# Opening of a state-space and MLP kernel: zero products first, first products split by tokens, one gate pass, and two tiles of B rows transposed by DMA

## Chip, cores and metric

One core of one Trainium2 chip. The metric is the device time of one execution in microseconds, lower is better. The time before is the median of five runs.

## The reference

For each of 2048 tokens `x` (width 1024) two branches are computed and mixed by a gate that is one number per token.

```python
g = _sigmoid((x * gate_w).sum(-1, keepdims=True))

# branch a: a diagonal complex state-space layer
Lam_bar = jnp.exp(dt * Lam)
B_bar = ((Lam_bar - 1.0) / Lam)[:, None] * Bmat
Bu = jnp.einsum("bld,pd->blp", x + 0j, B_bar)
for t in range(L):
    h = Lam_bar[None, :] * h + Bu[:, t, :]
y = 2.0 * jnp.einsum("blp,dp->bld", hseq, Cmat).real + x * Dskip

# branch b: layer norm and an MLP of width 3584
h = _gelu(jnp.einsum("bsd,df->bsf", _layernorm(x), w1) + b1)
b = jnp.einsum("bsf,fd->bsd", h, w2) + b2

out = g * a + (1 - g) * b
```

All inputs and the output are bf16.

## The kernel before

The program is a graph of tasks. Each task belongs to one engine (`pe`, `act`, `dve`, `pool`, or `sp` for DMA issue), has an estimated duration, a priority tuple and the buffers that it reads and writes. A list scheduler in `Graph` plays the graph through with those estimates and so fixes one order of instructions for each engine; on the chip every engine works through its order and waits on semaphores where a task needs another engine's or a DMA's result. Smaller priority tuples go first. A changed estimate (`DMAT_BW` is the assumed rate of transposing DMAs, `slack` an assumed delay of one task's input) changes the orders and nothing else.

The stages, in the order of the priorities:

1. **The opening.** `x` (tiles of 128 tokens) and `B_re`, `B_im` (tiles of 128 state channels, "p tiles") are needed with the width on the partitions. Tokens 0 to 511 are loaded as they are (`load_x`), transposed on TensorE (`t_x`, line 646) and copied out of PSUM by VectorE (line 650). The natural B rows of p tiles 0 to 3 are loaded to the region `RX` (`load_b0`, `load_b`), transposed on TensorE (`t_b`, line 662) and copied out by ScalarE (line 666). The other tokens come by DMA transposes of 512 tokens, 1 MB each (`xT_dma`, line 990), the B rows of p tiles 4 to 7 by DMA transposes of 256 KB (`bT_dma`, line 1079). The buffers of transposed B rows form a ring of five, `BQ`; the last two of them lie over `RX`.
2. **Constants.** Small vectors are loaded to `stg` (line 575), transposed in one TensorE instruction (line 693) and turned into the decay, its powers and tables by a long chain of small VectorE instructions with a few ScalarE functions (lines 696 to 814).
3. **Input products.** `bu_plain` computes the products of p tiles 0 and 1 with 512 tokens directly: eight matmuls of 512 columns for each part (real, imaginary), accumulated in one of six PSUM banks, which ScalarE empties (line 925). All later groups (`bu_group`) use a scheme with seven products of half-size blocks in place of eight (class `SG`, steps `p1` to `p7`): VectorE first forms sums of blocks (`b_sums` for B, `x_sums` for x with `ut1` to `ut4`; line 895), ScalarE copies or seeds partial results (lines 850 and 867). `ut4` and `bs4` are written over a block that the plain products read. The order of groups (p tile, token half) is (2,0), (3,0), (0,1), (1,1), ...
4. **Gate rows.** `z_gate` multiplies the columns `gate_w` and ones with x; the results of four token chunks lie in four strips of partitions of PSUM bank 7. It is done once for each token half (line 1046), ScalarE copies the rows out (line 1053), `z_move` sends them through DRAM to get one number per token on the partitions (lines 1062 and 1067). The ones give the sums for the layer norm. Later ScalarE applies tanh (line 1122) and VectorE makes `G` and `GM1`.
5. **Layer norm** (`ln_stats`; squares on ScalarE, line 1001; the norm on VectorE, line 1021), stored and read back by transposing DMAs.
6. **MLP**: blocks `m` (first product, gelu at lines 1295 and 1301) and `b` (second product, scaled by `GM1` at lines 1378 and 1381), accumulated in DRAM.
7. **The state recurrence** `ssm` (lines 1162 to 1189): filler work for VectorE with low priority between all these, 16 units of multiply, scan, multiply.
8. **The last stage** `y`: eight groups of the product with C, combined with the gate, the skip term and the MLP result (lines 1458 to 1480), and stored.

TensorE's instructions of the opening are chained one after the other in program order:

```python
t_x(0, (-0.8, 0), 7, [])
t_x(1, (-0.8, 1), 3, last_pe())
t_b(0, (-0.8, 2), (0,), (1, 2), last_pe())
t_x(2, (-0.8, 3), 0, last_pe())
t_x(3, (-0.8, 4), 7, last_pe())
t_b(0, (-0.79, 0), (1,), (1, 2), last_pe())
```

SyncE issues, in this order: x tiles 0 and 1, B re of p tile 0, x tiles 2 and 3, B im of p tile 0, the natural rows of p tiles 1 to 3, three DMA transposes of x, then x tiles 4 to 15 (for the layer norm) with the transposes of p tile 4 among them.

Of the kernel before, what the change touches and what calls it, by code (L numbers as in the profile page):

```python
# [7 lines left out]
F32 = mybir.dt.float32  # L8
# [14 lines left out]
DMAT_BW = 150e3  # L23
# [396 lines left out]
def build(nc, A_x, A_Lambda_re, A_Lambda_im, A_B_re, A_B_im, A_C_re, A_C_im, A_log_dt, A_Dskip,  # L420
# [25 lines left out]
    with es:  # L446
# [110 lines left out]
        for nm in ("SUM", "SSQ", "MEAN", "EX2", "MSQ", "VAR", "RSTD", "NMR", "Z", "TZ", "G", "GM1"):  # L557
            alloc_cols(nm, NTT)
# [20 lines left out]
        g.dma(P0, emit_cst_loads, NROW * 256, sem("d_cst"), writes=[b_stg], name="cst_loads", ndma=len(vecs), q="act")  # L579
# [73 lines left out]
        def t_b(pt, prio, ris=(0, 1), bks=None, ex=()):  # L653
            s = pt % 4
            for ri in ris:
# [8 lines left out]
                g.add("pe", 0.06 * DT, prio, em, reads=[AR.v(RX + s * 4096 + ri * 2048, [(1, D)]), b_ident], writes=[b_ps[bk]], name="bT%d.%d" % (pt, ri), extra=ex)  # L664
                o = AR.v(bqo(pt, 2 * ri), [(1, D)])
                first_a.append(g.add("act", c_act(D), prio, lambda e, o=o, bk=bk: e.activation(o.ap, V(PS16[bk], 0, [(1, D)]), AF.Copy),
                                     reads=[b_ps[bk]], writes=[o, b_ps[bk]], name="bTe%d.%d" % (pt, ri)))

        def load_b0(ri, ap):
            v = AR.v(RX + ri * 2048, [(1, D)])  # L670
            g.dma((-0.9, 1.5 + 2 * ri), lambda e: e.dma_start(out=v.ap, in_=ap[0:128, :]), 128 * D * 2,
                  sem("d_b0%d" % ri), writes=[v], name="bnat0.%d" % ri)

        load_b0(0, A_B_re)
        load_b0(1, A_B_im)
        BN[0] = AR.v(RX, [(1, 2 * D)])
        for k in range(4):
            load_x(k, (-0.9, k))
        for pt in range(1, 4):
            load_b(pt, (-0.85, pt))  # L680
# [4 lines left out]
        t_x(0, (-0.8, 0), 7, [])  # L685
        t_x(1, (-0.8, 1), 3, last_pe())
        t_b(0, (-0.8, 2), (0,), (1, 2), last_pe())
        t_x(2, (-0.8, 3), 0, last_pe())
        t_x(3, (-0.8, 4), 7, last_pe())
        t_b(0, (-0.79, 0), (1,), (1, 2), last_pe())  # L690
# [33 lines left out]
        dv("cos", lambda e: e.activation(C("C1", 0, n8), C("T3", 0, n8), AF.Sin, scale=TWO_PI), ["T3"], ["C1"], dur=0.3, eng="act", prio=P0)  # L724
        dv("ur0", lambda e: e.tensor_tensor(C("UR", 0, n8), C("R", 0, n8), C("C1", 0, n8), ALU.mult), ["R", "C1"], ["UR"])
# [189 lines left out]
        def bu_plain(pt, c):  # L915
# [4 lines left out]
            for ri in range(2):  # L920
                bk = (4, 5, 6, 0, 1, 2)[nxt("cbank", 6)]
                ws = [AR.v(bqo(pt, 2 * ri) + dt * 256, [(1, 128)]) for dt in range(DT)]
                q = mm("bu%d.%d.%d" % (pt, c, ri), bk, ws, [xt(dt, c) for dt in range(DT)], True)
# [6 lines left out]
        def b_sums(pt, q):  # L930
            def bv(i, dt=FP16):
                return AR.v(bqo(pt, i), [(1, 512)], dt)
            dve_tt("bs1_%d" % pt, q, bv(4), bv(2, BF16), bv(3, BF16), ALU.add, 512)
            dve_tt("bs2_%d" % pt, q, bv(5), bv(4), bv(0, BF16), ALU.subtract, 512)
            dve_tt("bs3_%d" % pt, q, bv(6), bv(0, BF16), bv(2, BF16), ALU.subtract, 512)
            dve_tt("bs4_%d" % pt, q, bv(2), bv(1, BF16), bv(5), ALU.subtract, 512)

        def x_sums(pr, q):
            def xv_(i, dt=FP16):
                return AR.v(xqo(pr, i), [(1, 2048)], dt)  # L940
            dve_tt("ut1_%d" % pr, q, xv_(4), xv_(2, BF16), xv_(0, BF16), ALU.subtract, 2048)
            dve_tt("ut2_%d" % pr, q, xv_(5), xv_(3, BF16), xv_(4), ALU.subtract, 2048)
            dve_tt("ut3_%d" % pr, q, xv_(6), xv_(3, BF16), xv_(2, BF16), ALU.subtract, 2048)
            dve_tt("ut4_%d" % pr, q, xv_(2), xv_(1, BF16), xv_(5), ALU.subtract, 2048)
# [52 lines left out]
        def ln_stats(c, prio):  # L997
            for i in range(TT):
# [3 lines left out]
                      reads=[xv], writes=[v_j, bc("SSQ%d" % k)], name="ln_sq%d" % k, extra=[first_a[3]])  # L1002
# [34 lines left out]
        def z_gate(pr):  # L1037

            cs = (2 * pr, 2 * pr + 1)
            xs = [[xt(dt, c) for c in cs] for dt in range(DT)]  # L1040

            def em(e):
                ins = None
                for dt in range(DT):
                    for i, c in enumerate(cs):
                        ins = e.matmul(bass.AP(PS[7], 32 * c * 512, [[512, 2], [1, CH]]), V(GWC, 2 * dt, [(1, 2)]), xs[dt][i].ap, start=(dt == 0), stop=(dt == DT - 1))
                return ins
            seq[0] += 1
            t = g.add("pe", 1.0, (1.0, seq[0]), em, reads=xs + [b_gwc], writes=[b_ps[7]], name="z%d" % pr, extra=pe_last)
            pe_last[:] = [t]  # L1050
            for c in cs:
                o = bass.AP(AR.h[F32], 32 * c * zrow + ZR // 4, [[zrow, 2], [1, CH]])
                g.add("act", c_act(CH), (1.0, seq[0]), lambda e, c=c, o=o: e.activation(o, bass.AP(PS[7], 32 * c * 512, [[512, 2], [1, CH]]), AF.Copy),
                      reads=[b_ps[7]], writes=[zr, b_ps[7]], name="ze%d" % c)

        def z_move(pr):

            prio = (1.0, seq[0])
            n = NTT // 2

            def em_st(e):
                return [e.dma_start(out=ZS[r, pr * 1024:(pr + 1) * 1024].rearrange("(c t) -> c t", c=2),
                                    in_=bass.AP(AR.h[F32], (64 * pr + r) * zrow + ZR // 4, [[32 * zrow, 2], [1, CH]])) for r in range(2)]
            g.dma(prio, em_st, L * 4, sem("d_zst%d" % pr, True), reads=[zr], writes=[b_zs[pr]], name="zst%d" % pr, ndma=2, q="pool").slack = 0.5
# [610 lines left out]
```

## Time and profile before

| | |
|---|---|
| median of 5 runs | 566.86 us (563.22 to 576.39) |
| the profiled execution's own time | 565.94 us |
| its span, first to last instruction | 564.2 us |
| TensorE busy in the span | 545.5 us |
| VectorE busy in the span | 519.9 us |
| ScalarE busy | 288.1 us |
| POOL busy | 94.6 us |
| first TensorE instruction | 3.32 us |
| HBM read, written | 60.98 MB, 48.38 MB |

Lines of the timeline read: start, length, engine, line of the kernel, operation, tiles written and read, shapes, count; in brackets the idle time of the engine before it and what ended it. Neighbouring instructions of one line are merged into one row. PE is TensorE's matmul, PEld its weight load, DVE VectorE, ACT ScalarE, SPq SyncE's DMA issue. A busy TensorE is not one at its best pace: the duration of like instructions has to be compared too.

### The profile page before, as it was taken

The page shows a single profiled execution, that of the slowest core. Times are in us where ns is not written, and L with a number is a line of the kernel's source. Part 1 is how long each engine was busy: PE and PEld are TensorE (multiplying, and loading weights), DVE is VectorE, ACT ScalarE, POOL GpSimd, SP SyncE. Part 2 cuts the span into 40 slices and gives each one's busy share as a digit, 9 for nine tenths or more (in the row PEclk, how much of TensorE's full clock was granted, in tenths as well). Part 3 has the DMA queues.
Part 4 walks back from the last instruction along what each step waited for, and adds up shares of the span by engine and source line. Part 5 has one row for each costly group of instructions (what it writes and reads, how often), then busy time and mean ns, then how long its engine had stood idle before and what let it go on. Part 6 is the DMA issues. An engine that isn't in the chain of part 4 may idle for free. (4 is left out here: it accounts for less than half of the span.)

```text
span 564.2 us, 7415 instructions
## 1 busy us (share of the span) xinstructions
PE 545.5 (97%) x2553; PEld 249.8 (44%) x2601; DVE 519.9 (92%) x894; ACT 288.1 (51%) x481; POOL 94.6 (17%) x153
## 2 busy tenths in 40 slices
PE   6999999989999999999999999999999999999995
PEld 5544444434444444444444444444444444444442
DVE  4899989999999999999999999999999788999952
ACT  3969989667774247774347663347663331111110
POOL 0225736530001110001110001120001110010100
PEclk9999999999999999999999999999999999999998
DMA  8995999767882564303998997997699799788421
GB/s 268 241 313 123 259 266 275 263 216 217 268 186 94 212 218 147 114 0 128 341 379 275 354 256 177 242 196 243 195 236 173 160 295 361 261 323 313 151 108 56
DMA packets 122287, 125.58 MB, mean 223 GB/s; under 512 B 70530, under 2 KB 99970, under 8 KB 121226
## 3 DMA queue, kind: packets, MB, share of 16 engines
q1 hardware_dynamic: 109136, 77.23, 48.9%
q0 software_dynamic: 13008, 47.87, 27.6%
q8 instruction: 20, 0.33, 0.2%
q14 instruction: 17, 0.14, 0.1%
q10 hardware_dynamic: 106, 0.02, 0.0%
HBM read 60.98 MB, written 48.38 MB: 194 GB/s over the span
## 5 line engine op out<-in xcount | busy, mean ns | idle before, releaser
L833 PE MATMUL ps<-ar 128*128 128x512 f16 (+1 forms) x1792 | 412.1, 379 | 6.1 <-ACT ar L850 1.6
L833 PEld LDWEIGHTS ps<-ar 128*128 128x128 f16 (+1 forms) x1832 | 178.5, 98 | 222.2 <-ACT ar L850 3.2
L831 PE MATMUL ps<-ar 128*128 128x512 bf16 (+1 forms) x632 | 156.2, 380 | 1.6 <-DVE ar L895 1.0
L895 DVE TENSOR_TENSOR ar<-ar 128x512 f16<-128x512 bf16 (+7 forms) x244 | 150.5, 652 | 7.4 <-DMA ar<-in_A_B_im_dram 2.4
L831 PEld LDWEIGHTS ps<-ar 128*128 128x128 bf16 (+1 forms) x640 | 62.2, 98 | 76.9 <-DVE ar L895 2.4
L1176 DVE TENSOR_TENSOR_SCAN ar<-cst,init,ar 128x256 bf16<-128x256 f32 x128 | 88.7, 734 | 0.4
L850 ACT ACTIVATE ar<-ps 128x512 f32<-128x512 f32 x100 | 58.8, 594 | 50.2 <-PE ps L831 37.7
L1162 DVE TENSOR_TENSOR ar<-ar 128x2048 bf16<-128x2048 bf16 x64 | 77.0, 1216 | 0.1
L867 ACT ACTIVATE ps<-ps 128x512 f32<-128x512 f32 x66 | 38.5, 583 | 68.2 <-PE ps L831 50.1
L1295 ACT ACTIVATE ar<-ps,cst 128x512 bf16<-128x512 f32 x56 | 38.4, 686 | 22.1 <-PE ps L833 21.4
L851 ACT ACTIVATE ar<-ps,cst 128x512 f32<-128x512 f32 x32 | 22.0, 687 | 45.5 <-PE ps L833 23.4
L1301 ACT ACTIVATE ar<-ar,cst 128x512 bf16<-128x512 f32 x56 | 40.0, 715 | 7.7 <-DVE ar L1299 7.7
L1378 ACT ACTIVATE ar<-ps,cst 128x512 f32<-128x512 f32 x32 | 22.0, 687 | 40.8 <-PE ps L833 40.8
L1165 DVE TENSOR_TENSOR ar<-ar 128x1024 bf16<-128x1024 bf16 x64 | 42.3, 684 | 0.3
L1299 DVE TENSOR_TENSOR ar<-ps,ar 128x512 f32<-128x512 f32 x56 | 38.2, 683 | 3.5 <-PE ps L833 3.1
L910 POOL DMA_DIRECT2D scr_u<-ar x32 | 24.9, 780 | 40.7 <-DVE ar L976 17.5
L1480 DVE SCALAR_TENSOR_TENSOR ar<-ps,cst,ar 128x512 bf16<-128x512 f32 x32 | 23.8, 745 | 7.4 <-PE ps L833 7.4
L1390 POOL DMA_DIRECT2D scr_ac<-ar x16 | 13.7, 859 | 88.4 <-DVE ar L1381 54.1
L1381 DVE SCALAR_TENSOR_TENSOR ar<-ps,cst,ar 128x512 f32<-128x512 f32 x32 | 23.7, 740 | 3.8 <-PE ps L833 3.7
L1388 POOL DMA_DIRECT2D scr_ac<-ar x16 | 8.5, 532 | 100.4 <-DVE ar L895 89.2
L1194 POOL DMA_DIRECT2D scr_h<-ar x16 | 9.3, 584 | 86.6 <-DVE ar L1165 86.5
L1487 POOL DMA_DIRECT2D out_dram<-ar x14 | 7.6, 544 | 84.3 <-DVE ar L1480 84.3
(104 smaller groups left out, 260.0 us busy)
## 6 DMA issues: line engine op xcount, KB each, us to landing
scr_ac<-ar POOLq DMA_DIRECT2D x32, 512.0 KB, 6.3
ar<-in_B_w_dram SPq DMA_DIRECT2D x21, 512.0 KB, 5.5
ar<-in_A_x_dram SPq DMA_DIRECT2D x32, 256.0 KB, 6.5
scr_u<-ar POOLq DMA_DIRECT2D x32, 256.0 KB, 4.9
ar<-scr_u SPq DMA_DIRECT2D x16, 512.0 KB, 5.0
scr_h<-ar POOLq DMA_DIRECT2D x16, 512.0 KB, 5.4
ar<-scr_h SPq DMA_DIRECT2D x8, 1024.0 KB, 7.2
ar<-scr_ac SPq DMA_DIRECT2D x16, 512.0 KB, 7.7
```

The costliest lines, as they stand in the source:

```text
L831: ins = e.matmul(V(PS[bk], 0, [(1, n)]), st[i].ap, mv[i].ap, start=(i == 0), stop=(i == K - 1))
L833: ins = e.matmul(V(PS[bk], 0, [(1, n)]), st[i].ap, mv[i].ap, start=False, stop=(i == K - 1), skip_group_check=True)
L850: return e.activation(o.ap, V(PS[bk], 0, [(1, 512)]), AF.Copy)
L867: g.add("act", c_act(512), (pb[0], q - 2), lambda e: e.activation(V(PS[b], 0, [(1, 512)]), V(PS[a], 0, [(1, 512)]), AF.Copy), reads=[b_ps[ ...
L895: g.add("dve", c_tt16(n), (pb[0], q), lambda e: e.tensor_tensor(o.ap, a.ap, b.ap, op), reads=[a, b], writes=[o], name=nm, extra=ex).slack ...
L910: g.dma((1.0, q), lambda e: e.dma_start(out=US[pt // 4, :, 4 * pr:4 * pr + 4, r0:r0 + T], in_=evv.ap), 2 * 128 * CH * 2, ssem("us", 2 * ks ...
L1162: g.add("dve", c_tt16(UE), pri(i), lambda e: e.tensor_tensor(o.ap, a.ap, tbl.ap, ALU.mult), reads=[a, tbl], writes=[o], name=nm + tag)
L1165: g.add("dve", c_tt16(UE // 2), pri(i), lambda e: e.tensor_tensor(o.ap, a.ap, b.ap, op), reads=[a, b], writes=[o], name=nm + tag)
L1176: lambda e, pt=pt, ri=ri, vin=vin, go=go: e.tensor_tensor_scan(go.ap, Cb("R", pt, T), vin.ap, V(INIT, pt * 2 + ri, [(1, 1)]), ALU.mult, AL ...
L1295: g.add("act", c_act(512, ap_operands=1), (10.0, q + 1), lambda e: e.activation(o.ap, V(PS[bk], 0, [(1, 512)]), AF.Gelu_apprx_tanh, bias=C ...
L1299: g.add("dve", c_dve(512), (10.0, q - 2), lambda e: e.tensor_tensor(sv.ap, V(PS[bk], 0, [(1, 512)]), sv.ap, ALU.add), reads=[b_ps[bk], sv] ...
L1301: g.add("act", c_act(512, psum=False, ap_operands=1), (10.0, q + 3), lambda e: e.activation(o.ap, sv.ap, AF.Gelu_apprx_tanh, bias=C("B1", ...
```

## The change

- Loads: B re of p tile 0 is issued first, then x tiles 0 and 1, B im, x tiles 2 and 3, and the natural rows of p tile 1. Those of p tiles 2 and 3 are no longer loaded; their transposed rows come by `bT_dma`, between the DMA transposes of x. The constants' loads go from ScalarE's queue to POOL's.
- TensorE's opening begins with six products of zeros; the direct products of p tile 0 with the first 512 tokens are done in halves of 256 tokens between the transposes (`part`). The PSUM copies of p tile 0's rows are shared by VectorE and ScalarE.
- The gate rows of all four token chunks are made in one pass within group (3,0), `ut4` of the first token half after it.
- The gate's tanh is replaced by a power of e on POOL and a reciprocal on VectorE; a small gelu instruction stands early in ScalarE's order.
- The scheduler's numbers: a higher rate for transposing DMAs, and 5 us of slack for two of the four B sums of p tiles above 4.

```diff
-DMAT_BW = 150e3
+DMAT_BW = 200e3
...
-        g.dma(P0, emit_cst_loads, NROW * 256, sem("d_cst"), writes=[b_stg], name="cst_loads", ndma=len(vecs), q="act")
+        g.dma((-0.5, 0), emit_cst_loads, NROW * 256, sem("d_cst"), writes=[b_stg], name="cst_loads", ndma=len(vecs), q="pool")
...
+                w = D // 2 if halves else D
+                if halves:
+                    o = AR.v(bqo(pt, 2 * ri) + D, [(1, w)])
+                    g.add("dve", 0.36, prio, lambda e, o=o, bk=bk: e.tensor_copy(o.ap, V(PS16[bk], w, [(1, w)])),
+                          reads=[b_ps[bk]], writes=[o, b_ps[bk]], name="bTd%d.%d" % (pt, ri))
+                o = AR.v(bqo(pt, 2 * ri), [(1, w)])
...
-        load_b0(0, A_B_re)
-        load_b0(1, A_B_im)
+        for k, ri in ((None, 0), (0, None), (1, None), (None, 1), (2, None), (3, None)):
+            if ri is None:
+                load_x(k, (-0.9, k + 1 if k < 2 else k + 2))
+            else:
+                load_b0(ri, (A_B_re, A_B_im)[ri])
         BN[0] = AR.v(RX, [(1, 2 * D)])
-        for k in range(4):
-            load_x(k, (-0.9, k))
-        for pt in range(1, 4):
-            load_b(pt, (-0.85, pt))
+        load_b(1, (-0.85, 0))
...
+        v_zero = AR.v(B2B, [(1, CH)])
+        g.add("dve", 0.1, (-2.0, 0), lambda e: e.memset(v_zero.ap, 0.0), writes=[v_zero], name="zero")
+
+        def warm(n, bk, w):
+            def em(e):
+                ins = None
+                for i in range(n):
+                    ins = e.matmul(V(PS[bk], 0, [(1, w)]), AR.v(B2B, [(1, 128)]).ap, AR.v(B2B, [(1, w)]).ap, start=True, stop=True)
+                return ins
+            g.add("pe", n * w * 0.00084, (-0.8, -1), em, reads=[v_zero], writes=[b_ps[bk]], name="warm", extra=last_pe())
+
+        def part(t0, n, ri):
+            if True:
+                ws = [AR.v(bqo(0, 2 * ri) + dt * 256, [(1, 128)]) for dt in range(DT)]
+                xs = [AR.v(xqo(0, 0) + dt * 1024 + 2 * t0, [(1, n)]) for dt in range(DT)]
+                bk = 4 + ri
...
+                        ins = e.matmul(V(PS[bk], t0, [(1, n)]), ws[dt].ap, xs[dt].ap, start=(dt == 0), stop=(dt == DT - 1))
...
-        t_x(0, (-0.8, 0), 7, [])
+        warm(6, 6, CH)
+        t_b(0, (-0.8, 2), (0,), (1, 2), last_pe(), True)
+        t_x(0, (-0.8, 0), 7, last_pe())
         t_x(1, (-0.8, 1), 3, last_pe())
-        t_b(0, (-0.8, 2), (0,), (1, 2), last_pe())
+        t_b(0, (-0.8, 2), (1,), (1, 2), last_pe(), True)
+        part(0, 256, 0)
         t_x(2, (-0.8, 3), 0, last_pe())
         t_x(3, (-0.8, 4), 7, last_pe())
-        t_b(0, (-0.79, 0), (1,), (1, 2), last_pe())
+        part(0, 256, 1)
+        part(256, 256, 0)
+        t_b(1, (-0.8, 5), (0,), (1, 2), last_pe())
+        part(256, 256, 1)
+        t_b(1, (-0.8, 5), (1,), (1, 2), last_pe())
...
+        g.add("act", 0.3, (3.0, 0), lambda e: e.activation(C("KF2", 0, 1), C("MHALF", 0, 1), AF.Gelu_apprx_tanh), ... name="gelu_tab")
...
+            sl = 5.0 if pt > 4 else 0.0
+            dve_tt("bs1_%d" % pt, q, bv(4), bv(2, BF16), bv(3, BF16), ALU.add, 512, sl)
...
+            dve_tt("bs3_%d" % pt, q, bv(6), bv(0, BF16), bv(2, BF16), ALU.subtract, 512, sl)
...
-        def z_gate(pr):
+        def z_gate():
...
-                    for i, c in enumerate(cs):
-                        ins = e.matmul(bass.AP(PS[7], 32 * c * 512, [[512, 2], [1, CH]]), V(GWC, 2 * dt, [(1, 2)]), xs[dt][i].ap, start=(dt == 0), stop=(dt == DT - 1))
+                    for c in range(NCH):
+                        ins = e.matmul(bass.AP(PS[7], 32 * c * 512, [[512, 2], [1, CH]]), V(GWC, 2 * dt, [(1, 2)]), xs[dt][c].ap, start=(dt == 0), stop=(dt == DT - 1))
...
-        for pt in range(1, 4):
-            t_b(pt, (0.9, pt))
-        for c in range(1, NCH):
-            xT_dma(c, (-0.6 + 0.1 * c, 0))
...
+        xT_dma(1, (-0.84, 0))
...
+        bT_dma(2, (-0.83, 0))
+        bT_dma(3, (-0.35, 0))
+        xT_dma(2, (-0.4, 0))
+        xT_dma(3, (-0.3, 0))
...
-            if c == 1:
-                z_gate(0)
-                z_move(0)
             for pt in range(2):
                 bu_plain(pt, c)
-        x_sums(0, seq[0])
+        x_sums(0, seq[0], (0,))
...
             if (pt, pr) == (0, 1):
-                z_gate(1)
-                z_move(1)
                 x_sums(1, seq[0])
...
             cur.p6()
+            if n == 1:
+                z_gate()
+                z_move()
+                x_sums(0, seq[0], (1,))
             cur.p2()
...
-        g.add("act", 0.3, (5.0, 0), lambda e: e.activation(C("TZ", 0, NTT), C("Z", 0, NTT), AF.Tanh, scale=0.5), ...
+        g.add("pool", 0.5, P0, lambda e: e.memset(C("EULER", 0, NTT), 2.718281828459045), writes=[bc("EULER")], name="euler")
...
+        gp("nz", lambda e: e.tensor_scalar(C("TZ", 0, NTT), C("Z", 0, NTT), -1.0, 0.0, ALU.mult, ALU.add), zb, "TZ")
+        gp("ez", lambda e: e.tensor_tensor(C("EZ", 0, NTT), C("EULER", 0, NTT), C("TZ", 0, NTT), ALU.pow), [bc("TZ"), bc("EULER")], "EZ")
+        gp("e1", lambda e: e.tensor_scalar(C("TZ", 0, NTT), C("EZ", 0, NTT), 1.0, 0.0, ALU.add, ALU.add), [bc("EZ"), bc("TZ")], "TZ")
+        g.add("dve", 0.1, (5.0, 0), lambda e: e.reciprocal(C("G", 0, NTT), C("TZ", 0, NTT)), reads=[bc("TZ")], writes=[bc("G")], name="G")
```

## The prediction

> **What bounds the kernel now.** I read the page first, then the table of windows, the timeline of the opening, the waits, and the chain that ended last.
>
> ```profile
> PE 545.5 (97%) x2553; PEld 249.8 (44%) x2601; DVE 519.9 (92%) x894; ACT 288.1 (51%) x481; POOL 94.6 (17%) x153
> ...
> DVE  4899989999999999999999999999999788999952
> ```
>
> TensorE is busy 545.5 of 564.2 us, so 18.7 us is all its idle time: 3.3 before the first transpose, some 6.8 after the last product, and the rest in a few gaps. Nothing outside TensorE's own work can give much. VectorE is the second bound: nine tenths or more in nearly every slice, with little room when TensorE gets quicker.
>
> ```profile
> 3.32 1.03 PE L646 MATMUL ps<-ident,ar 128*128 128x128 bf16 x8 [3.32 <-DMA ar<-in_A_x_dram]
> ...
> 7.12 1.91 PE L646 MATMUL ps<-ident,ar 128*128 128x128 bf16 x16
> ...
> 12.34 1.06 PE L662 MATMUL ps<-ident,ar 128*128 128x128 bf16 x16
> 13.23 1.89 PE L831 MATMUL ps<-ar 128*128 128x512 bf16 x8
> 14.96 0.61 PE L662 MATMUL ps<-ident,ar 128*128 128x128 bf16 x8
> ...
> 20.45 1.89 PE L1046 MATMUL ps<-ar,gwc 128*2 128x512 bf16 x16
> 22.27 8.81 PE L831 MATMUL ps<-ar 128*128 128x512 bf16 x39
> 30.98 2.75 PE L833 MATMUL ps<-ar 128*128 128x512 f16 x12
> ```
>
> This is TensorE's opening. Before 10 us sixteen transposes take 1.70 us start to start (7.12 to 8.82); at 12.34 sixteen take 0.89 (12.34 to 13.23). The pace doubles between 10.4 and 12.3 us, after work without a gap since 6.29 (the wait for the first B rows ends there). The stretch at 22.27 holds the last 32 plain products and the first 8 of group (2,0): that group begins at 30.98 - 8 x 0.216 = 29.2 us (0.216: the eight products at 13.23 are followed at 14.96, 1.73 us later).
>
> ```profile
> 100.16 1.28 ACT L1122 ACT_TABLE_LOAD   x1
> ...
> 102.21 1.90 PE L833 MATMUL ps<-ar 128*128 128x512 bf16 x8 [0.90 <-ACT ar L850]
> ...
> 126.28 3.63 PE L833 MATMUL ps<-ar 128*128 128x512 f16 x16 [1.45 <-ACT ps L867]
> ```
>
> ScalarE loads a table for tanh, and TensorE waits 0.90 us behind it. The 1.45 us gap comes some 5 us after the like load for the first gelu (at 120.30).
>
> ```profile
> 430.00:470.00 40.00, 39.79 (x183) 18.09 (x185) 32.67 (x41) 11.35 (x18) 6.53 (x8) 1.00 0.87 218
> 470.00:537.00 67.00, 65.73 (x301) 29.79 (x306) 66.55 (x90) 10.31 (x18) 6.52 (x12) 1.00 0.78 278
> ```
>
> Columns: stretch, length, busy time of PE, PEld, DVE, ACT and POOL, then clock and DMA. From 470 to 537 VectorE has 0.45 us idle; at 521 TensorE waits for it:
>
> ```profile
> 519.15 1.19 DVE ar L1459
> 520.34 0.61 DVE ar L895
> 520.95 0.05 issue
> 521.00 1.90 PE ps L831 x8
> ```
>
> These are pieces of the chain that ended last: it leaves TensorE for VectorE between 510 and 521 us.
>
> **The opening, part by part.** Each load takes SyncE about 0.45 us to issue. The first six land at 3.3, 4.6, 6.25, 7.0, 7.9 and 8.6 us (issue plus time to landing), the next two at 8.95 and 9.9. I keep these times and put the new order on them: B re, x0, x1, B im, x2, x3, B1 re, B1 im.
> Zero products: six of 512 columns at the slow pace (0.106 per 128 columns, so 0.427 each) are 2.6 us, from about 1.0 (first VectorE memset at 0.87) to 3.6. They lie in the 3.3 us wait for the first load and cost 0.3 at most, which the wait for x0 at 4.6 swallows. What they may bring is the early pace. No row shows it, so two ends:
> Slow until 11.3 as now: B re 3.6-4.5, x0 4.6-5.5, x1 6.3-7.15, B im 7.15-8.0, first half product (8 x 0.213) 8.1-9.8, x2 and x3 9.8-11.5, then fast: three half products of 0.88, two transposes of B1 at 0.45, constants 0.15, to 15.2. The 48 plain products left, at 0.216, are 10.4: group (2,0) at 25.6.
> Fast from 4.6: the same list waits for landings and for x1's eviction (0.69 at line 650) until 7.75, ends at 13.3, and group (2,0) begins at 23.7.
> Before, without the first gate pass (1.8), it is 29.2 - 1.8 = 27.4. The gain is 1.8 to 3.7; I take 2.8, the middle. It contains the four transposes of p tiles 2 and 3 that leave (4 x 0.45 to 0.6).
> [...]
>
> Gate rows: 20.45 to 22.27 and 39.70 to 41.53 are 3.65 us for two passes of 16. In one pass two strips already run at the price of one (16 of them in 1.89). Four at once would be 1.8; if the weight loads (16 in 1.38 us, line 1046) bind, 32 take 2.75; with no more overlap than now 3.65. I take 2.2: gain 1.45, ends 0 and 1.85.
> The pass now lies in group (3,0), and ut4 of the first x half, in place over what the pass reads, must follow it. Behind ut4 waits p4 of group (2,0). Cover: p2 and p3, 8 x 0.216 = 1.7 us. ut4 takes 0.96 to 1.22 (line 895, 2048 wide) after at most one such instruction ahead of it: 0 to +1.2, I take +0.2. The pass also waits for all x by DMA: SyncE issues the three 1 MB transposes in 4.8 us each (the first 7.4, behind loads), with two pairs of B rows (1.24 + 1.40 each) between. Two fewer pairs of loads are ahead, so it starts at 4.6, not 6.75: first issue done near 11.9, B2 14.6, second x 19.4, B3 22.0, third x 26.8, landing 2 to 3.5 us later. Wanted: second x chunk at 17 to 19 (lands near 15), B2 at 24, third x at 32 to 33: all covered.
> x4 to x15 and p tile 4's transposes come behind this: x4 is issued near 29.4 instead of 23.8. Cover: the norm that reads them starts at 59.1 and its first product past 114; price if the cover is gone, the 5.6 us.
>
> Moved off queues: five constant loads go from ACT to POOL. POOL takes 0.55 to 0.8 each (lines 1062, 910), so about 1.4 to 5.5, landing by 8.5; the constants' transpose comes at 15. ACT sheds four evictions of 1.03, half of two, three gate evictions of 0.59 and tanh; idle time of ACT, no gain. One cost sits here: the constant chain on VectorE starts at 15.2 instead of 10.1.
>
> **Later parts.** Without tanh, and with gelu's table loaded in the opening (1.28 us, between evictions of 0.6 that come every 1.7 us; without that cover 1.3): the 0.90 gap goes. The 1.45 gap hangs also on VectorE's add ahead of a gelu, so little of it. I take -1.2, ends 0 and -2.35. The planner's 5 us for B sums of p tiles over 4: VectorE waited 2.39 us for a B row at 73.81, TensorE 0.73 after it: -0.3, ends 0 and -0.73. The gate on POOL (three small operations, up to 1.4 each as at line 1015) is due at 166.9, line 1378: nothing.
>
> **VectorE's share.** TensorE would come 5.5 us earlier (2.8 + 1.45 + 1.2), VectorE's chain 5.1 later, and two half copies add 0.7 (half of line 650 each): 11.3 us less room. Idle that lateness fills by itself: its waits for TensorE, 4.9 in 430:470 and about 3.0 between 183 and 424, and the 2.4 of the B row: 10.3. So at least 1.0 returns as TensorE stalls in the 470 to 537 stretch. If VectorE's fixed order regains little of it (about half, 5.4), 5.9 returns. I take +1.6, ends 0 and +5.9.
>
> Sum: -2.8 - 1.45 + 0.2 - 1.2 - 0.3 + 1.6 = -3.95, and +0.3 for p tile 3's B rows, whose margin is thin (below): -3.65. The profiled execution took 565.94 us (span 564.2, 1.7 around it): **562.3 us**, 0.64% less. The median of the runs shown is 566.86, 0.2% above that execution, and the runs reach from 563.22 to 576.39; I don't correct for it. About 1%, 5.7 us, is what a measurement here tells from no change.
>
> **Rivals.** All of it arrives and VectorE keeps up: -3.7 - 1.85 - 2.35 - 0.73 = -8.6, 557.3 us. For it: VectorE idles 7.3 us in 430:470. Against: 0.45 in the stretch after.
> VectorE takes the bound over: -2.8 - 1.45 - 1.2 - 0.3 + 0.5 + 5.9 = +0.65, 566.6 us. For it: the chain through VectorE at 510 to 521. Against: its waits for TensorE go by themselves when it is late.
> Slower: B rows of p tile 3 land late. Their region is that of the natural B rows, so they wait for B1's transposes, and may be issued behind the third x chunk: imaginary row issued near 25.5. Group (3,0) wants its sum at 30.3. At 3.5 us to landing all is well; the longest such landing in the trace is 12.3 (line 1079): 37.8, a stall of 7.5, +3.9 in all, 569.8 us. It decides from a landing after 34.0. For it: the median for imaginary rows is 10.1. Against: those were queued behind ten x loads.
> The zero products may also do nothing to the pace: 563.3, inside the forecast.
>
> **How the numbers follow.** Forecast 0.53, all arrives 0.27, VectorE takes over 0.11, late B rows 0.09. Faster by over 1% (under 560.3): 0.27 and 0.06 of the forecast, 0.33. Slower by over 1%: 0.09, nearly all of the last. Within: 0.58. The range goes from the first rival, 557, to 568, part of the way to the last; the forecast's own is 559.5 to 565.5.
>
> **What would show it.** Right: TensorE's first matmuls near 1 us, transposes at 0.61 per eight before 8 us or at the latest by 11.3, group (2,0) at 23.7 to 25.6, one gate pass of 1.8 to 2.75, no table load after 40 us, 2 to 3 us more TensorE idle in the last 100 us. Wrong: group (2,0) after 27, a gap at group (3,0), a gate pass of 3.6, or VectorE's idle in 430:470 unchanged.

## Result and profile after

The change makes the kernel slower by 0.8%: 572.32 us median (565.02 to 584.24, 44 runs) against 566.25 us (561.02 to 576.39, 79 runs of the kernel before on the same chips). The ratio is 1.008 with a 95% interval of 1.0057 to 1.0104; it leaves out executions that lie far above the fastest of their kernel, which is why it is below that of the medians. The prediction was 562.3 us and at most 568.

The profiled execution took 581.03 us (span 579.3), so it is one of the long ones; a second trace of the same kernel (run e9 below) took 576.37 us (span 574.6) and loses its time in the same places. Lines of the kernel have moved: 646 and 662 (transposes) are the same, 831 and 833 (products) are 872 and 874, 850 and 867 are 891 and 908, 895 is 936, 1046 is 1095, 1219 (the transposing loads of the normed x, called xn here) is 1273, 1480 is 1534. The zero products are line 700, the half products line 714.

Of the page, the sums by engine, VectorE's slices and the granted clock:

```profile
PE 550.4 (95%) x2544; PEld 250.1 (43%) x2591; DVE 522.4 (90%) x897; ACT 280.7 (48%) x473; POOL 99.4 (17%) x160
...
DVE  4899797799999999999988999999999979999853
...
PEclk9999799799999999999999999999999999997998
```

TensorE is now idle 28.9 us (579.3 - 550.4; it was 18.7). The clock row has three dips, at the slices near 65, 110 and 530 us; before, it had none until 560.83 us. VectorE has holes at the same early slices.

The timeline of TensorE's opening:

```profile
1.24 2.74 PE L700 MATMUL ps<-ar 128*128 128x512 bf16 x6 [1.24 <-DVE ar L818]
...
4.63 1.44 PE L646 MATMUL ps<-ident,ar 128*128 128x128 bf16 x16
6.08 0.62 PE L662 MATMUL ps<-ident,ar 128*128 128x128 bf16 x8
...
12.84 12.03 PE L872 MATMUL ps<-ar 128*128 128x512 bf16 x54 [0.16 <-ACT ar L971]
25.70 2.75 PE L874 MATMUL ps<-ar 128*128 128x512 f16 x12 [0.82 <-DVE cst L786]
...
32.87 1.90 PE L1095 MATMUL ps<-ar,gwc 128*2 128x512 bf16 x32 [0.97 <-DMA ar<-in_A_x_dram]
```

The row that stood at 30.98 stands at 25.70, and the 32 gate products take 1.90 us: in this trace the opening did what was forecast. The rival of late B rows didn't occur: the imaginary row of p tile 3 is issued at 20.45, ahead of the third x chunk, and lands at 25.04. TensorE's waits from 60 to 540 us, the three longest:

```profile
PE ps L874 <- ACT ar L891: 6.1, 1, 6.1
PE ps L874 <- DVE ar L1534: 3.8, 1, 3.8
PE ps L874 <- ACT ar L1029: 3.3, 1, 3.3
```

Before, the longest wait in this stretch was 1.45 us. The timeline around the longest, all engines:

```profile
94.61 9.98 SPq L1273 DMA_TRANSPOSE ar<-scr_xn  x2
...
97.48 0.17 DVE L1239 TENSOR_TENSOR fxt<-ar,cst 128x8 f32<-128x8 bf16 x1
...
104.87 1.23 DVE L936 TENSOR_TENSOR ar<-ar 128x2048 f16<-128x2048 bf16 x1 [7.22 <-DMA ar<-scr_xn]
...
107.41 0.60 ACT L1029 ACTIVATE ar<-ps 128x512 f32<-128x512 f32 x1 [6.87 <-DVE ar L1031]
107.90 1.08 ACT L891 ACTIVATE ar<-ps 128x512 f32<-128x512 f32 x2
...
108.55 3.60 PE L874 MATMUL ps<-ar 128*128 128x512 bf16 x8 [6.05 <-ACT ar L891]
```

VectorE comes in its fixed order to the first sum of normed x at 97.65 and waits 7.22 us for the transposing loads. Behind the sum stand the copies that ScalarE and then TensorE wait for. The last row holds a second price: eight products in 3.60 us, 0.43 each where 0.22 is usual. The table of windows shows it:

```profile
103.92:107.34 3.42, 0.00 (x0) 0.00 (x0) 2.47 (x4) 0.00 (x0) 0.35 (x1) 1.00 1.04 208
107.34:110.75 3.41, 2.20 (x6) 0.83 (x7) 3.41 (x6) 2.06 (x4) 2.80 (x5) 0.50 1.14 303
110.75:114.16 3.41, 3.41 (x10) 1.20 (x9) 3.38 (x8) 0.81 (x2) 1.40 (x3) 0.50 0.86 333
```

After the five busy times and their counts comes the granted clock: half for 6.83 us after the gap. TensorE works for 2.20 + 3.41 = 5.61 us of it, so the wait of 6.05 us costs up to half of that, 2.8 us, more (an estimate from the two paces, 0.43 and 0.22).

The table of windows for the two stretches that the prediction watched:

```profile
430.00:470.00 40.00, 39.79 (x183) 18.14 (x186) 39.00 (x54) 12.06 (x18) 6.63 (x8) 1.00 0.86 198
470.00:537.00 67.00, 62.33 (x273) 27.41 (x276) 61.45 (x83) 9.57 (x16) 6.28 (x11) 0.95 0.86 296
```

VectorE's idle time in the first fell from 7.3 to 1.0 us, as lateness would have it; in the second TensorE now idles 4.7 us, where it was 1.3.

By stretches, TensorE's idle time in the first trace before and in e9: 60 to 95 us 0.9 and 2.5, 95 to 110 us 0.95 and 8.9, 470 to 540 us 1.3 and 3.95. That is 12.2 us more. In e9's two half-clock stretches (6.83 and 3.41 us; the granted clock is 0.86 from 95 to 110 us, 0.93 from 110 to 130 and 0.98 from 470 to 540) TensorE is busy for 7.3 us, half of which, 3.6, is lost; together 15.8. The span is only 10.4 longer, so some 5.4 us were gained elsewhere. Against the second trace of the kernel before (e10 below: span 560.0, idle 0.2, 0.2 and 1.5 us in the same stretches) the same sum is 13.5 + 3.6 - 14.6: some 2.5 us gained.

### The profile page after: what moved, and what is told of

Read it like the earlier page. It is cut to its first block, busy times and chain, and to the rows that moved or that the text cites. A ratio compares the mean times of both kernels' runs of the same rounds, so it can differ in the third digit from the quotient of the medians.

```text
span 579.3 us, 7382 instructions
## 1 busy us (share of the span) xinstructions
PE 550.4 (95%) x2544; PEld 250.1 (43%) x2591; DVE 522.4 (90%) x897; ACT 280.7 (48%) x473; POOL 99.4 (17%) x160
## 3 DMA queue, kind: packets, MB, share of 16 engines
q0 software_dynamic: 13104, 47.88, 27.3%
## 4 chain that ended last, share of the span: by engine, by line
PE 69%; DVE 12%; DMA 7%; SPq 5%; POOL 2%; issue 2%; ACT 1%; DVEq 0%; ACTq 0%; POOLq 0%
PE ps L874 54%; PE ps L872 15%; DMA ar<-in_A_x_dram 4%; DMA ar<-in_B_w_dram 2%; DVE ar L936 2%; SPq L1040 2%; DVE ar L1513 2%; DVE ar L1534 2%; SPq L1273 1%; SPq L1123 1%; DVE ar L1532 1%; DMA ar<-scr_xn 1%; DVE ar L1512 1%; DVE ar L1230 1%; DVE ar L1216 1%
## 5 line engine op out<-in xcount | busy, mean ns | idle before, releaser
L874 PE MATMUL ps<-ar 128*128 128x512 f16 (+1 forms) x1799 | 417.7, 383 | 18.4 <-ACT ar L891 6.1
L936 DVE TENSOR_TENSOR ar<-ar 128x512 f16<-128x512 bf16 (+6 forms) x244 | 150.1, 653 | 13.4 <-DMA ar<-scr_xn 7.2
L872 PE MATMUL ps<-ar 128*128 128x512 bf16 (+1 forms) x610 | 153.5, 385 | 1.4 <-DMA ar<-scr_h 0.4
```

The costliest lines, as they stand in the source:

```text
L872: ins = e.matmul(V(PS[bk], 0, [(1, n)]), st[i].ap, mv[i].ap, start=(i == 0), stop=(i == K - 1))
L874: ins = e.matmul(V(PS[bk], 0, [(1, n)]), st[i].ap, mv[i].ap, start=False, stop=(i == K - 1), skip_group_check=True)
L936: g.add("dve", c_tt16(n), (pb[0], q), lambda e: e.tensor_tensor(o.ap, a.ap, b.ap, op), reads=[a, b], writes=[o], name=nm, extra=ex).slack ...
```

## Experiments

All kernels whose part of the change is undone are planned anew by the scheduler, so every engine's order moves with them. Those marked "orders kept" change what an instruction does, or the place of a named few, and nothing else in any engine's order.

**One part undone (e1 to e4).** The planner's rate back, two gate passes, B rows by TensorE, tanh on ScalarE.

```diff
-DMAT_BW = 200e3
+DMAT_BW = 150e3
```

> The changed kernel with one number undone: the planner's rate for transposing DMAs is 150e3 again (it changes engine orders only). Theory R (rate): the higher rate makes the planner place VectorE's sums of the normed x before the transposes that feed them have landed, and VectorE's 7.2 us wait at 105 us and TensorE's 6.05 us gap behind it come from that: without it that gap is under 1.5 us, and the time falls 5 to 9 us below the changed kernel's, to 0.992 to 1.000 of the kernel before. Theory G (one gate pass), theory B (B rows by DMA) and theory P (gate's power on POOL) say the transposes themselves are late, whatever the planner assumes: a gap of 3 us or more stays near 100 us, and the ratio stays 1.004 or more.

Measured 569.38 us, 1.0036 (1.0007 to 1.0065). The order gives the first sum more room (xn third landing 94.8, sum at 102.6), the gap at 105 us is gone as theory R has it, but the time is over its range: TensorE waits elsewhere for VectorE's sums. From 3 to 545 us the two longest waits in total are

```profile
PE ps L872 <- DVE ar L936: 5.2, 3, 3.6
PE ps L874 <- DVE ar L936: 2.8, 4, 1.9
```

e2, the functions of the gate from before:

```diff
+            if c == 1:
+                z_gate(0)
+                z_move(0)
```

> The changed kernel with the two gate passes of before, at their old places, and all four x sums of the first half together. Theory G: one late pass lets the sums for the layer norm of all 16 token tiles arrive at once, so that POOL's small operations and the stores of normed x come in a bunch, u stores wait behind them (TensorE's gap at 64 us) and the transposes run against them (gap at 105): without it both gaps are under 1 us and the ratio to before is 0.990 to 0.998, although the second pass costs 1.8 us again. Theories R, B and P: at least one of the gaps at 64 and 105 stays, ratio 1.004 to 1.012.

569.99 us, 1.0048 (1.0016 to 1.0081). The gap near 64 us stays (2.08 us; the granted clock of the run is 0.990), the one near 105 is gone, and the time is over theory G's range.

```diff
-        bT_dma(2, (-0.83, 0))
-        bT_dma(3, (-0.35, 0))
+        for pt in range(2, 4):
+            t_b(pt, (0.9, pt))
```

> The changed kernel with the B rows of p tiles 2 and 3 loaded as they are and transposed on TensorE, as before. Theory B: their DMA transposes push the loads of x4 to x15 back by 8.6 us (32.4 for 23.8), with them the squares, the norm and its transposes: without them x4 is issued near 27, the gap at 105 is under 2 us, and the time falls 3 to 7 us in spite of 1.8 us more of transposes on TensorE: ratio 0.996 to 1.003. Theories R, G and P: the gaps stay and the 1.8 us come on top, ratio 1.006 to 1.014.

564.47 us, 0.9956 (0.9924 to 0.9988), no gap over 1.5 us after the opening. It made theory B the leader. The same kernel in another job:

> The version with the B rows of p tiles 2 and 3 by TensorE once more, to see whether it really beats both kernels. In its order the gate's power stands at 93 us, behind the stores of normed x. If its first 0.9956 holds: 0.993 to 0.998. If that was the luck of one job, as 1.0008 and 1.0033 of its near relatives suggest: 0.998 to 1.003.

567.43 us, 1.0021 (0.9977 to 1.0065). So the first figure is not a gain that is shown to last, and no version here is shown to beat the kernel before.

e4, tanh and its two VectorE instructions from before in place of the power on POOL:

> The changed kernel with the gate's tanh on ScalarE again and without the early gelu instruction (the whole gate part undone). Theory P: the power on POOL (3.16 us at 62.8, with two smaller operations) holds the u stores behind it and makes the gap of 3.35 us at 64 us: without it that gap is under 1 us, and the time falls 3 to 6 us, less about 1.2 us for the two table loads that come back: ratio 0.998 to 1.004. Theories R, G and B: the gap near 105 us stays and the tables cost 1 to 2 us, ratio 1.008 to 1.014.

568.82 us median, 561.36 to 574.77; ratio 0.9948 (0.9907 to 0.999), while the median is no lower than the 568.06 of the kernel before in this job. The time is inconclusive. The trace speaks against theory P: without the gate's power on POOL, the gap of 3.06 us at 64.9 is there, the four loads of xn take SyncE 32.1 us, VectorE stands idle 9.89 us ahead of its first sum, and TensorE has a gap of 7.28 us at 111.6.

**One part alone, and two undone (e5 to e8).**

```diff
-        for pt in range(1, 4):
-            t_b(pt, (0.9, pt))
+        t_b(1, (0.9, 1))
...
+        bT_dma(2, (-0.83, 0))
+        bT_dma(3, (-0.35, 0))
```

> The kernel before with one part of the change alone: the B rows of p tiles 2 and 3 transposed by DMA, in the places of SyncE's order that the change gives them. Theory B (the DMA'd rows are what costs: they hold SyncE and the DMA engines while the x chunks wait): the third x chunk lands 3 to 5 us later than 25.91 and x4 is issued 6 us or more later than 23.83, TensorE gets at least one gap of over 2 us between 30 and 110 us, and the time is 0.5 to 1.2% above before. Rival S (no single part; the whole planned order came out badly): within 0.3% of before or faster, since four transposes and four evictions leave TensorE and ScalarE.

568.82 us, 1.0033 (0.9998 to 1.0069). x4 is issued at 33.83, the third x chunk lands at 34.08, and TensorE waits 2.9 us at 36.1. Theory B's signs are there, at under half the price of the whole change, with an interval that reaches 1.

e6 is the changed kernel with B rows by TensorE, two gate passes, tanh and the planner's old numbers:

> The opening alone: zero products, the new order of the first loads, token-split first products, constant loads on POOL; B rows by TensorE, two gate passes, tanh and the planner's costs as before. Theory B: the opening keeps what it won, the first f16 product begins at 27 to 28.5 us with a first gate pass ahead of it (30.05 before), and the time is 0.3 to 0.7% below before. Rival S: what the opening wins is lost again in VectorE's order, ratio 0.999 to 1.005.

574.25 us (565.33 to 578.03, six runs, no ratio). The row of the first twelve f16 products stands at 30.77: with a gate pass ahead of it as before, and no earlier than before (30.98). TensorE has a gap of 4.8 us at 104.6, and the four loads of xn take 30.6 us. That speaks against theory B: B rows by TensorE, and a loss is back.

> All of the change but two parts: B rows by TensorE again and tanh on ScalarE again. Theory B with the gate on POOL as a second, smaller loss (POOL's 3.16 us power no longer stands ahead of the u stores): ratio 0.990 to 0.995, below the 0.9956 that B rows by TensorE alone gave. If the gate on POOL is nothing, as the prediction had it: 0.995 to 0.998, and the 0.90 and 1.45 us waits behind table loads are back.

573.20 us (561.16 to 583.99, six runs): one program gives nearly the shortest and nearly the longest time of all kernels here. That is neither case of the expectation. The gaps lie at 106.1 (5.2 us) and 113.2 (3.4 us), and VectorE waits 9.4 us for xn, without DMA transposes of the B rows of p tiles 2 and 3 and without the gate's power on POOL.

e8 leaves out the zero products (`warm(6, 6, CH)`) of e3:

> B rows by TensorE, and no zero products at the start. If the zero products bring the early full pace: the clock record rises between 8 and 11.5 us instead of 5.1, the first f16 product comes 1.5 to 3 us later than 26.38, ratio 0.998 to 1.002. If they do nothing: the rise stays near 5 us or the later rise costs under 0.5 us, and the ratio stays at 0.994 to 0.997.

566.85 us, 1.0008 (0.998 to 1.0037). In its timeline the pace rises between 7.42 and 8.76 us, without any zero product, after transposes almost alone:

```profile
4.45 2.18 PE L646 MATMUL ps<-ident,ar 128*128 128x128 bf16 x16
6.43 1.06 PE L662 MATMUL ps<-ident,ar 128*128 128x128 bf16 x8
7.42 1.50 PE L713 MATMUL ps<-ar 128*128 128x256 bf16 x8
8.76 1.06 PE L646 MATMUL ps<-ident,ar 128*128 128x128 bf16 x16
...
28.17 2.76 PE L872 MATMUL ps<-ar 128*128 128x512 f16 x12 [0.50 <-ACT ps L906]
```

With the zero products that last row stands at 28.00 in e3, where the pace rose at 5.1 us (the expectation's 26.38 is no row of its trace), and at 28.18 in e18. With the B rows by TensorE they buy 0.2 us at most in these traces; 0.9956 against 1.0008 is no price of them, as e18 has 1.0021. In the changed order no run left them out.

**Both kernels once more (e9, e10).**

> The changed kernel once more, for a second trace of it. If its loss sits in fixed places (feed of VectorE by the xn transposes near 105 us, u stores near 62 us), both gaps of TensorE come again, whatever their size, with the clock at half after them; if the first trace was an accident of one execution, the time is near 566 and neither gap is over 1.5 us.

576.37 us. VectorE's wait for xn is 9.62 us, TensorE's gap behind it 7.76; the one near 63 us is 1.3, and the clock stays full there. The loss near 105 us is fixed in place, not in size.

> The kernel before once more, for a second trace. If its order leaves the xn transposes more room (the first sum of normed x stood 6.8 us behind the landing it needs), TensorE has no gap of over 2 us between 60 and 115 us here either; if not, the transposes come late here too, with a gap of VectorE that ends on scr_xn.

561.70 us, with no gap of over 1.2 us after the opening. ScalarE loads its two tables here too (at 97.27 and 117.42), and TensorE waits under 0.1 us behind either.

**Orders kept (e11 to e13, e17).** The first takes the transposing from the B rows, the second from the normed x:

```diff
-lambda e, ...: e.dma_start_transpose(out=o.ap, in_=ap[pt * 128:(pt + 1) * 128, :])
+lambda e, ...: e.dma_start(out=n.ap, in_=ap[pt * 128:(pt + 1) * 128, :]) if pt < 4 else e.dma_start_transpose(...)
```

> The changed kernel with every engine's order kept as it is, and the four DMA transposes of the B rows of p tiles 2 and 3 replaced by plain loads of the same bytes (so their data lie untransposed, which changes the output). Theory B (these transposes take SyncE's time and the DMA engines'): SyncE issues the four in 0.45 us each in place of 1.3 to 2.7, x4 is issued 3 to 6 us before 32.40, the third x chunk lands before TensorE wants it, and the ratio falls from 1.008 to 1.000 or less. Theory F (VectorE's fixed order wants the normed x before the DMA chain can bring it, whatever the B rows do): x4 comes earlier and the ratio stays at 1.004 to 1.009, with the gap near 105 us.

573.22 us, 1.0107 (1.0048 to 1.0165). x4 is issued at 28.08 in place of 32.40, and VectorE still waits 10.64 us for xn. Theory B falls as the cause of the loss.

```diff
-e.dma_start_transpose(out=o.ap, in_=XNS[r0:r0 + 512, dh * 512:(dh + 1) * 512])
+e.dma_start(out=o.ap, in_=XNS[r0:r0 + 512, dh * 512:(dh + 1) * 512].rearrange("(a p) d -> p a d", p=128))
```

> The changed kernel with every engine's order kept, and the first four transposes of normed x replaced by plain loads of the same bytes (data untransposed, which changes the output). Theory F: all four are landed within 15 us of the first issue, VectorE's wait for scr_xn (7.22 us) and TensorE's gap of 6.05 us with the half clock behind it go, and the ratio falls by 0.007 to 0.012, to 0.996 to 1.001. Theory B: the loss is made before 70 us, the ratio falls by 0.003 at most.

567.33 us, 1.0041 (0.9994 to 1.0088): 5.0 us below the changed kernel's median, and 5.9 below e11 in the same job, with every order the same. By the ratios it is 0.004 below the changed kernel's 1.008: less than theory F's 0.007 to 0.012, with intervals that overlap. Its waits of TensorE from 60 to 540 us begin with another one:

```profile
PE ps L874 <- DVE ar L1534: 3.8, 1, 3.8
PE ps L874 <- ACT ps L908: 1.4, 2, 1.1
PE ps L874 <- ACT ar L1029: 1.3, 1, 1.3
```

The gap of 6 us is gone. The view of the loads' line shows why, first of the changed kernel, then of e12, with the shortest, median and longest issue in ns and, below, the time to landing:

```profile
L1273 SPq DMA_TRANSPOSE ar<-scr_xn x4: 1861/5758/13658, 77.3 to 102.7; - x4
...
  DVE ar L936: 7.2, 1
...
DMA to landing us min/median/max: 4.7/11.4/22.0
```

```profile
L1273 SPq DMA_DIRECT2D ar<-scr_xn x4: 368/790/1223, 74.6 to 82.5; - x4
...
DMA to landing us min/median/max: 7.0/9.1/10.3
```

Four transposes hold SyncE for 27.3 us where four plain loads of the same bytes are through in 9.1. The next run makes the gate's power cheap:

```diff
-C("TZ", 0, NTT), ALU.pow)
+C("TZ", 0, NTT), ALU.mult)
```

> The changed kernel with every engine's order kept and the gate's power on POOL (3.16 us at 62.80, ahead of u stores and of the stores of the normed x) replaced by a product of the same shape, so the gate's values are wrong. If POOL's power is what makes the stores of normed x late (first at 66.1 to 69.6 us against 59.4 and 60.6 before): first store 2 to 4 us earlier, VectorE's wait for scr_xn shorter by as much or gone, ratio 1.002 to 1.006 against before. If the slow transposes themselves are (second and third issued in 8 to 13 us each beside twelve stores): the store comes earlier and the wait stays over 4 us in most runs, ratio 1.007 to 1.010.

568.25 us (564.69 to 583.36), 1.003 (0.9997 to 1.0064). The number is that of the first case, the mechanism isn't: the first store stands at 66.86, no earlier than in e9 (66.35). Yet VectorE waits only 0.66 us for xn in this trace, because the same four transposes took 19.5 us here. The next run moves the gate with its power kept:

```diff
+        po[:] = [t for t in po if t not in gate]
+        k = [t.name for t in po].index("xns11") + 1
+        po[k:k] = gate
```

> The changed kernel, full output, with one thing moved in its orders: POOL's three gate operations stand behind the twelfth store of normed x in place of ahead of the first, and VectorE's two that use them behind the sums of normed x. If POOL's power ahead of the stores is the step that failed: first store 3 to 4 us earlier, VectorE's wait for scr_xn gone in the trace, ratio 1.000 to 1.004 as with the cheap gate (1.003). If the transposes' own pace decides: the wait for scr_xn stays in the trace and the ratio is 1.007 to 1.010. What is left over 1.000 is then VectorE's lateness behind TensorE's gap near 515 to 528 us, 3.5 to 3.8 us in every trace of this order, with the half clock behind it.

571.85 us, 1.0124 (1.0074 to 1.0174). First store 66.47, wait for xn 2.47 us in the trace. Moving POOL's power out of the way did not bring the time back, so it isn't shown to be the cause. e13's trace had quick loads; whether the cheap product made them so is not shown.

**The sums moved (e14 to e16).**

```diff
-dve_tt("xT1_%d" % c, q, xq(3), b12, xq(0), ALU.subtract, 2048, ex=ex)
+dve_tt("xT1_%d" % c, q, xq(3), b12, xq(0), ALU.subtract, 2048, 0.0 if late else 10.0, ex=ex)
```

> The changed kernel with the planner told that the first sums of normed x may begin only 10 us after their transposes have landed; TensorE's order and VectorE's up to 97 us stay as they are. Theory F (the loss is VectorE's fixed order meeting a late DMA chain): VectorE does its other work while the chain is under way, its wait for scr_xn is under 2 us, TensorE's gap near 108 us and the half clock behind it go, ratio 0.996 to 1.003. If the late chain itself sets the time (the products that use the sums wait in place of the sums): the gap moves to the first products of the MLP, ratio 1.005 to 1.010.

572.09 us, 1.0084 (1.0037 to 1.013). No wait for xn, but the sums run at 114, and the products wait at 130.7 instead:

```profile
PE ps L874 <- DVE ar L936: 4.5, 1, 4.5
```

> The kernel before with the same 10 us. Its first sum already stands 6.8 and 8.3 us behind its landings in two traces, so theory F gives a ratio of 0.996 to 1.001, with fewer long executions; a ratio over 1.004 would say that the delayed sums have a price of their own, to be taken off the reading of the run beside this one.

572.30 us, 1.0102 (1.0058 to 1.0147), with a gap of 5.7 us at 126. In these six executions the move alone costs the kernel before 1%.

> The version with the B rows by TensorE (ratio 0.9956 when measured alone) with the same 10 us. Theory F: there the first sum stood 2.5 us behind its landing and did not wait, so no change, 0.993 to 0.998; below 0.993 if it too lost executions to that wait.

569.01 us, 1.0033 (0.9989 to 1.0076), gap 3.4 us at 126.5. So the sum has a narrow place: before it the loads aren't there, behind it the first products of the MLP wait. It isn't VectorE's order alone: the chain that ends in the sums leaves each of the three orders little room.

The chain in the traces, in us. "Wanted" is when VectorE is ready for the first sum, "room" that less the third landing, which this sum needs.

| | first xn store | four loads issued | third landed | wanted | room |
|---|---|---|---|---|---|
| before | 60.62 | 72.97 to 90.74 | 90.86 | 97.63 | +6.8 |
| before again (e10) | 59.42 | 69.13 to 84.67 | 84.89 | 93.18 | +8.3 |
| after | 69.57 | 77.29 to 104.58 | 104.84 | 97.65 | -7.2 |
| after again (e9) | 66.35 | 74.75 to 104.55 | 104.93 | 95.33 | -9.6 |
| B rows plain (e11) | 67.62 | 76.08 to 107.19 | 107.56 | 97.11 | -10.5 |
| gate moved (e17) | 66.47 | 73.60 to 99.71 | 99.56 | 97.11 | -2.5 |
| gate cheap (e13) | 66.86 | 76.00 to 95.51 | 95.57 | 94.94 | -0.6 |
| xn plain (e12) | 66.11 | 74.56 to 83.66 | 91.06 | 95.10 | +4.0 |

In the changed order the chain starts 6 to 10 us later, and its transposing loads take 20 to 31 us in place of 15 to 18, while the sum is wanted when it was wanted before. The room of 6.8 us is gone, and the wait grows with the loads: 19.5, 26.1, 27.3, 29.8 and 31.1 us of them go with waits of 0.7, 2.5, 7.2, 9.6 and 10.6.

## Why the prediction was wrong

**The opening: near in its sum, wrong in its parts.** Against 2.8 us forecast, the twelve-product row came 30.98 - 1.8 - 25.70 = 3.5 us earlier, and in e9 (26.80) 2.4. The kernel before has this row at 29.79 in e10, where two products take 0.59 us, the full pace, at 10.72 already, while in the first trace the clock rose at 11.28; from there the gain is 2.3 and 1.2. e3 and e18, with all of the new opening and B rows by TensorE, have it at 28.00 and 28.18, only 1.2 and 1.0 earlier by the first sum, and e6 gains nothing. The rest goes with the four transposes that left. The zero products are worth 0.2 us at most by e8, in the order with B rows by TensorE. What the early pace is worth in the changed order is not shown: the row stands at 25.70 with a rise at 4.94 us, at 26.57 in e12 and 26.80 in e9, and at 28.19 in e11 (B rows plain), where the sixteen half products that begin at 8.79 in the page's execution begin at 11.23 in spite of the zero products. (The work ahead of the rise before was not quite "without a gap since 6.29": TensorE waits 0.33 us at 10.38.) Work that was mostly transposes did go before the full pace: in e8 TensorE was busy for 3.32 of the 3.41 us from 4.97 to 8.38, of which 0.96 were products and the rest transposes, and sixteen transposes took 2.18 us at 4.45 and 1.06 at 8.76.

**The gate pass: right.** 1.90 us for 32 products, the lower end (1.8). The wait for the third x chunk, costed as covered, is 0.97 us in the trace (it landed at 32.83), none in e9 and 4.4 in e14.

**The gains together: right only against the trace they were read from.** 2.8 + 1.45 - 0.2 + 1.2 + 0.3 is 5.55 us; by the stretches above 5.4 arrived against that trace, and 2.5 against e10. No table is loaded after 20.03 us, and the waits of 0.90 and 1.45 us are gone. But e10 doesn't have these waits either, though it loads both tables: they came and went with the execution, and the 1.2 us taken for them was no lasting loss of the kernel before.

**The cover of the norm: the step that failed.** The prediction said of the later x4 "the norm that reads them starts at 59.1 and its first product past 114". The first to read the chain is not a product but VectorE's sum at 97.6, and its room was 6.8 us. Nor is it x4 that uses the room up (e11). The chain starts late at POOL, here in the timeline after:

```profile
61.21 2.82 DVE L1071 TENSOR_SCALAR ar<-ar,cst 128x1024 bf16<-128x1024 bf16 x6
...
62.80 3.16 POOL L1177 TENSOR_TENSOR cst<-cst 128x16 f32<-128x16 f32 x1
65.82 1.62 POOL L951 DMA_DIRECT2D scr_u<-ar  x2
...
69.57 1.96 POOL L1073 DMA_DIRECT2D scr_xn<-ar  x3
```

VectorE has six tiles normed by 64.03, and the first store follows at 69.57; before, the first two are normed from 59.08 to 60.09 and the first store stands at 60.62. In POOL's new order the norm's small operations of several chunks, the gate and the u stores (of the input products, line 951) stand ahead of it, and the loads behind it are slow. I costed POOL's queue only for the constants and called the gate on it nothing, due at 166.9; it ran at 62.8 in the midst of this chain. Moving it away (e17) does not bring the chain back, so no price of its own is shown, but looking it up would have led to the place. The planner's rate of transposing DMAs, which had no term at all, lets the planner set the sum earlier against its loads; e1 takes that back and the gap with it. What was 0 in the sum is worth 5.0 us by the medians of e12, some 2.2 (0.004) by the ratios.

**VectorE's share: right in kind, at the far end in size.** I took +1.6 of 0 to 5.9. TensorE's wait for the last stage (line 1534) is 3.0 to 3.8 us in each of the six traces of this order, against 0.96 and 1.16 before (there on a sum, line 895); with up to 1.7 us for a half-clock stretch of 3.41 behind it this is some 3.5 to 4.5. No run takes this wait away, so its price is an estimate from the traces.

**Half clock: no term.** Every gap was costed at its length. In the page's execution TensorE is busy for 16.9 us of three stretches of 6.83 us at a granted clock of 0.50, which costs 8.5 by the two paces; in e9 two stretches cost 3.6.

5.0 (chain, its half clock included) + 4 (VectorE) - 5.55 gives +3.5 against the +6.1 of the medians. TensorE's extra 1.6 us of idle time between 60 and 95 us is part of the rest; with the 2.5 us gained against e10 in place of 5.55 the sum would be +6.5. No run decides between the two.

**What stays open.** Why four transposing loads of 0.5 MB are through in 15 us in one execution and in 31 us in another, and in one order in 19.5 (e13) or 29.8 (e9); a run without stores beside them wasn't tried. And which part of the change gave the planner the worse order: every part undone makes a new one, and e3 and e18, one program, differ by 0.65% between two jobs.

## What to carry to other kernels

Follow a chain that is moved (store, load, sum) to its first reader on any engine and take that reader's room from the trace; where two fixed orders meet, a gain on one side is spent there unless the other comes earlier too. Cost a wait of TensorE with the clock behind it (here 6.05 us of waiting and up to 2.8 more). Take a second trace before a short wait is counted as something to gain. Where a planner orders the work, test one part with the orders kept, and measure a promising version twice.

## What the hardware showed

The granted clock falls to half behind some of TensorE's waits. In the page's execution it falls at 62.97, 107.34 and 527.18 us, during waits of 3.35, 6.05 and 3.79 us that end at 64.12, 108.55 and 528.16, and is full again at 69.79, 114.17 and 534.00. TensorE is busy for 5.67, 5.62 and 5.62 us of these three stretches. Eight products of 512 columns take 1.90 us at 517.29, at full clock, and 3.59 at 528.16, at half.

In e6 it is 0.50 from 101.86 to 105.27, around the gap at 104.6.

The length of a wait alone did not tell whether that happened. In e1 TensorE's longest wait from 20 to 540 us is 3.6 us, and its granted clock over the whole span is 0.998: room for some 2 us of half clock in all (an estimate from that mean). From 60 to 95 us TensorE is idle for 2.59 us in e17, with a granted clock of 0.95, and for 2.48 in e9 and in e12, with 1.00. What else decides is not shown here.

The zero products are not the only way to an early pace. With them the clock is full from 4.94 us on in the page's execution. Without them it is from 11.28 in the kernel before, and in e8 the pace rises between 7.42 and 8.76.
